# Two more stages of the first MLP compute their third token tile's first layer by half-tile block products

## The chip, the cores and the metric

The kernel runs on one core of one Trainium2 chip. The metric is the device time of one execution, in microseconds (us). The kernel before takes 558.34 us (median of 3 runs, 557.42 to 559.12). In what follows PE is TensorE, DVE is VectorE, ACT is ScalarE, POOL is GpSimd and SP is the engine whose queue issues most of the loads.

## The reference

Retention attention gives `x`, a matrix of 1536 tokens by 512, and two MLPs follow it. All inputs are float64 in memory; the result is float32.

```
for each of the 12 blocks of 64 positions:             # 2 batches, 8 heads of 64
    out[block] = ((qb kb^T) * Dmask) vb + (qb * lam_pow) kv_state
    kv_state   = lam_block * kv_state + (kb * rev_pow)^T vb
x = out as [1536, 512]
h = max(x @ w_in, 0);  x = (h * h) @ w_out             # first MLP,  w_in [512, 2048], w_out [2048, 512]
h = x @ w_in2;  out = max(0.01 h, h) @ w_out2          # second MLP, same sizes
```

## The kernel before

**Products.** A fp32 value is kept as a pair of fp32r values, a high part (`hi`, `xhi`, `g0h`) and the remainder (`lo`, `xlo`, `g0l`). One product is three matmuls that add up in PSUM: hi·hi, hi·lo and lo·hi. All of them are issued in `three` (L612).

**Tiles and stages.** The head of the program does retention in 12 units of 128 tokens. Then each MLP `l` (0 or 1) runs in four stages `s` of 512 of the 2048 hidden columns; a stage is written (l, s). The tokens are three tiles of 512, called tile 0, 1 and 2. A stage does in this order:

- `first_pair`: the first layer of tiles 0 and 1 together, as one 2 by 2 block product computed by seven block products and sums (a Strassen-like scheme) in place of eight. It needs sums of weight blocks (`sw`) and of token blocks (`tt`: `t2`, `t3`, `t4`). For each half `h` of the stage's columns the products go to PSUM banks A, B, C and D; `s1[h]` is a copy of bank A made on ACT (L758), `s2[h]`, `r22[h]` and the rest are sums made on DVE (`plus`, L752). `put` hands a finished block to `activate` (L530 to L541): ReLU, square, and the split into `g0h`/`g0l` (tile 0) or `g1h`/`g1l` (tile 1). The subtraction for the low part is L541 on DVE.
- `second` of tile 0: the second layer, 4 outputs of 12 matmuls. Its result is copied from PSUM (L798 on ACT) and added to a spill area in DRAM by a GpSimd DMA.
- the first layer of tile 2: `first`, 48 matmuls of 512 columns, in MLP 0; `first_halves` in MLP 1, which splits tile 2 into two halves of 256 tokens and uses seven block products again: 7 products x 2 halves of the hidden columns x 6 matmuls = 84 matmuls of 256 columns. `halves_sums` makes the sums of token blocks (`u2`, `u3`, `u4`, and one in place in `xhi[2]`/`xlo[2]`).
- `second` of tile 1 and of tile 2.

Stage (0,3) ends with tile 2's first layer placed among the second layer of tile 1.

**Weights.** A fetch (`fetch`, L65 on SP) brings 1 MB of float64 words into one of two `raw` buffers. `converting` (L131 to L177) turns it into a pair: an absolute value on ACT (L143), four DVE steps in place in one of two `hb` buffers (L146, L147, L149, L152), a cast to the high part on ACT (L168) and a subtraction for the low part on DVE (L170). The last of the four DVE steps frees the `raw` buffer, so the next fetch is issued behind it. W1 halves additionally get their block sums (`weight_sums`, or `sums_in_place` for stages after (1,0)). W2 halves go to one of three places `w2h0` to `w2h2` in turn up to stage (1,0); a place is free when the second layer that reads it is done.

**What sets the order.** PE's order is the program's own (a manual schedule). The other engines' orders come from the tile scheduler: it goes by program order and by priority; `tc.keep_in_program_order` pins an instruction. The conversions are generators; a `yield` in the parts of a stage lets `convert` take one step of the oldest conversion or, if fewer than two are at work, begin another. A set `opened` holds a conversion back until a buffer's former reader is placed. Every instruction waits in its engine's queue behind the one ahead of it.

Of the kernel before, what the change touches and what calls it, by code (L numbers as in the profile page):

```python
# [20 lines left out]
def tile_retention_then_two_mlps(  # L21
# [56 lines left out]

    order = [(0, 0, 0, 0), (0, 0, 0, 1), (0, 0, 1, 0), (0, 0, 1, 1)]
    stages = [(l, s) for l in range(2) for s in range(NS)]  # L80
    halved = (1, 0)
    for before, stage in zip(stages, stages[1:]):
        if before != stages[0]:
            order.append((*before, 1, 1))
        own = [(*stage, 1, 0), (*stage, 0, 0), (*stage, 0, 1)]
        order += own[1:] + own[:1] if stage > halved else own
    order.append((*stages[-1], 1, 1))
    todo = list(order)
    fetched, at_work = [], []
# [42 lines left out]
    def converting(pin):  # L132
        key, r = fetched.pop(0)
        l, s, n, h = key
        k = 4 if n == 0 else 2
        words = r.bitcast(U32).rearrange("p (f t) -> p f t", t=2)
        w_lo, w_hi = words[:, :, 0], words[:, :, 1]
        ve = nc.vector
        hb = cv.tile([P, 4 * CW], U32, tag="hb", name="hb", bufs=2)
        hf = hb.bitcast(F32)  # L140
        half = hb.bitcast(U16).rearrange("p (f t) -> p f t", t=2)[:, :, 0]

        step = nc.scalar.activation(hf, w_hi.bitcast(F32), AF.Abs)  # L143
        if pin or key == order[1]:
            tc.keep_in_program_order(step)
        yield ve.tensor_scalar(out=hf, in0=hf, scalar1=2.0 ** -15, scalar2=122368.0, op0=ALU.max, op1=ALU.min)  # L146
        yield ve.tensor_scalar(out=hb, in0=hb, scalar1=3, scalar2=0x3FFFFFFF,  # L147
                               op0=ALU.logical_shift_left, op1=ALU.bitwise_and)
        yield ve.scalar_tensor_tensor(out=hb, in0=w_hi, scalar=0xC0000000, in1=hb,  # L149
                                      op0=ALU.bitwise_and, op1=ALU.bitwise_or)  # L150

        step = ve.scalar_tensor_tensor(out=half, in0=w_lo, scalar=2.0 ** -29, in1=half, op0=ALU.mult, op1=ALU.add)  # L152
        fetch()
        yield step
        if (l, s) != stages[0] and n == 0 and (l, s) <= halved:
# [9 lines left out]
        place = (2 * stages.index((l, s)) + h) % 3 if (l, s) <= halved else (2, 0)[h]  # L165
# [5 lines left out]
        if n == 0 and (l, s) > halved:  # L171
            yield from sums_in_place(key, f"sw{h}", hf)
        if (l, s) == stages[-1] and n == 1:
            while ("sums", h) not in opened:
                yield None
            parts = spare if h else None
            yield from sums_in_place(key, "t2", hf, parts)  # L177

    def convert(pin=False):
        for piece in list(at_work):  # L180
            step = next(piece[1], False)
            if step is False:
                at_work.remove(piece)
            elif step is not None:
                if pin:
                    tc.keep_in_program_order(step)
                return
        if fetched and len(at_work) < 2:
            begin(pin)

    def begin(pin=False):
        key = fetched[0][0]
        at_work.append((key, converting_halves() if key == order[0] else converting(pin)))
        step = next(at_work[-1][1])
        if pin:
            tc.keep_in_program_order(step)
# [11 lines left out]
    def retention(ctx_att, att):  # L208
# [180 lines left out]
        for i in range(n_units):  # L389
# [23 lines left out]
                output(i, range(2, NP))  # L413
            else:
                state(i)
                for _ in range({8: 2, 9: 2, 10: 1}.get(i, 0)):
                    convert(pin=True)
                output(i)
            if i + 1 < n_units:
                scale_k(i + 1)  # L420
            if i == 11:
# [90 lines left out]
    def halves_sums(j):  # L512
# [8 lines left out]
        for n, src in ((2, c), (4, d), (1, a), (3, b)):  # L521
# [3 lines left out]
            if j == 0:  # L525
                pool, tag = {2: (wp, "w2h1"), 3: (wp, "w2l1"), 4: (cv, "rb")}[n]
                uu[n] = pool.tile([P, 2, 2, TT // 2], F32R, tag=tag, name=f"u{n}", bufs=1)
            split(uu[n][:, 0, j], uu[n][:, 1, j], src)

    def activate(l, src, r, ghi, glo, one=False):  # L530
        if l == 0 and one:
# [113 lines left out]
    def first_halves(l, s, t=2):  # L645
# [65 lines left out]
            sums_last(2)  # L711
        else:
            opened.update((*stages[stages.index((l, s)) + 1], 0, h) for h in range(2))


    def first_pair(l, s):
        last = (l, s) == stages[-1]
        new_g(l, s, 0)
        new_g(l, s, 1)
        ve = nc.vector  # L720
# [21 lines left out]
        def put(h, src, r, i, t):  # L742
            m = 2 * h + i
            with tc.high_priority(offset=400 if t == 0 else 0):
                if last:
                    activate_last(t, m, src)
                else:
                    activate(l, src, r, g[t][0][:, m], g[t][1][:, m], src is r and (l, s) != stages[1])

        def plus(h, out, where, other):  # L750
            with tc.high_priority(offset=400):
                ve.tensor_tensor(out=out, in0=ps[h, where], in1=other, op=ALU.add)  # L752

        both = range(2)
        for h in both:
            b = product(h, "A", "A11", "B11")
            s1[h] = plain()
            nc.scalar.copy(s1[h], b)  # L758
            yield (l, s) != stages[1]
        for h in both:  # L760
            product(h, "B", "S2", "T2")
            s2[h] = plain()
            plus(h, s2[h], "B", s1[h])
            yield (l, s) != stages[1]
        for h in both:
            product(h, "D", "A22", "T4")
            yield (l, s) != stages[1]
        if last:
            opened.add(("sums", 0))
        for h in both:  # L770
# [6 lines left out]
        for h in both:  # L777
            product(h, "C", "S1", "T1")
            plus(h, r22[h], "C", r22[h])
            yield (l, s) != stages[1]  # L780
        for h in both:
            put(h, product(h, "A", "A12", "B21", False), plain(), 0, 0)
            yield last
# [4 lines left out]
        for h in both:  # L788
            put(h, r22[h], r22[h], 1, 1)
            put(h, s2[h], s2[h], 0, 1)  # L790
        if last:
            sums_last(0)
            sums_last(1)
# [104 lines left out]
    def second(l, s, t, ms=range(4)):  # L898
        last = s == NS - 1
        for m in ms:  # L900
# [34 lines left out]
                opened.add(("pair", l, s))  # L935
            if t == 2 and m == 3:
                i = stages.index((l, s))
                mid = stages.index(halved)
                then = ((i + 1, 1), (i + 2, 0)) if i < mid - 1 else ((i + 1, 0), (i + 1, 1))
                opened.update((*stages[n], 1, h) for n, h in then)  # L940
            if (l, s, t) == (1, 0, 0) and m < 2:
                halves_sums(m)
            yield not (last and t == 1 and m > 1)

    def stage(l, s):
# [7 lines left out]
                            second(l, s, 2)]  # L953
        if (l, s) == stages[-1]:
            return parts + [first_halves(l, s)] + [second_last(s, t) for t in range(NTILE)]
        tile_2 = first_halves if l else first
        return parts + [second(l, s, 0), tile_2(l, s, 2), second(l, s, 1), second(l, s, 2)]

    begin()
# [1 line left out]
    with tc.manual_schedule(engines={mybir.EngineType.PE}):  # L961
        for l, s in stages:
            for part in stage(l, s):
                for room in part:
                    if room is not False:
                        convert(pin=(l, s) == stages[1])


# [23 lines left out]
```

## Time and profile before

| what | value |
|---|---|
| median of three runs | 558.34 us |
| the profiled execution | 558.2 us |
| span in its trace | 556.4 us |
| PE busy / DVE busy / ACT busy | 549.7 / 436.2 / 300.3 us |
| matmuls of `three` (L612), without a gap in the chain | 2472 |
| POOL busy | 87.8 us |

The span is what the trace of the profiled execution covers; 1.8 us of that execution lie around it. Busy time is that in which an engine has an instruction at work; matmuls overlap, so a start-to-start distance says more of PE than the length of one. A timeline row gives the start, the length, the engine, the line, what is written and what is read, and in brackets the idle time before it and what ended it.

### The profile page before, as it was taken

The numbers are of one execution on the slowest core, as the hardware profiler recorded it, in microseconds if no ns is written. First come the engines' busy times: TensorE is split into PE (matmuls) and PEld (weight loads), VectorE is DVE, ScalarE is ACT, GpSimd is POOL, SyncE is SP. The second block draws the span as 40 slices with busy tenths as digits, with TensorE's granted clock in tenths as the row PEclk, the third lists the DMA queues.
The fourth block names the chain that finished last, engine by engine and source line by source line (L and its number), as shares of the span: only waits on it lengthen the run. The fifth ranks groups of instructions, "written<-read, shape, count | busy, mean of one in ns | idle before, by whom it ended". The sixth has DMA issues, their size and how long they took to land.

```text
span 556.4 us, 8706 instructions
## 1 busy us (share of the span) xinstructions
PE 549.7 (99%) x3386; PEld 471.2 (85%) x3386; DVE 436.2 (78%) x643; ACT 300.3 (54%) x482; POOL 87.8 (16%) x99
## 2 busy tenths in 40 slices
PE   8999999999999999999999999999999999999997
PEld 7998888888888888888888889888898889888997
DVE  5668999996776895639999986969276964967987
ACT  3444799546783456553366374654364464646620
POOL 4965000000203101220000000000213011220041
PEclk9999999999999999999999999999999999999999
DMA  9998245443459716584413221263628643660434
GB/s 211 226 228 249 77 151 171 182 140 114 58 170 181 195 12 142 143 157 137 151 57 115 76 95 58 75 227 121 96 30 164 196 99 54 74 78 1 165 139 151
DMA packets 68056, 71.86 MB, mean 129 GB/s; under 512 B 39856, under 2 KB 43952, under 8 KB 68016
## 3 DMA queue, kind: packets, MB, share of 16 engines
q1 hardware_dynamic: 60816, 58.60, 33.8%
q0 software_dynamic: 6912, 12.59, 16.1%
q8 instruction: 26, 0.43, 0.3%
q10 hardware_dynamic: 288, 0.14, 0.1%
q14 instruction: 14, 0.11, 0.1%
HBM read 49.29 MB, written 22.02 MB: 128 GB/s over the span
## 4 chain that ended last, share of the span: by engine, by line
PE 96%; DVE 2%; DMA 1%; ACT 1%; issue 0%; SPq 0%; DVEq 0%; ACTq 0%
PE ps L612 90%; PE ps L301 2%; PE ps L363 1%; PE ps L361 1%; PE ps L280 1%; DMA k<-in_k 1%; PE ps L332 1%; DVE Pm L306 0%; ACT kqT L284 0%; DVE xlo L69 0%; DVE hb L124 0%; DVE st L344 0%; ACT kqT L288 0%; SPq L65 0%; DVE hb L128 0%
## 5 line engine op out<-in xcount | busy, mean ns | idle before, releaser
L802 POOL DMA_DIRECT2D spill<-f x48 | 42.6, 893 | 402.3 <-ACT f L798 402.3
L798 ACT COPY f<-ps 128x512 f32<-128x512 f32 x72 | 41.7, 586 | 68.3 <-PE ps L612 68.1
L612 PE MATMUL ps<-xlo,w1h 128*128 128x512 f32 (+1 forms) x190 | 69.3, 368 | 0.0
L612 PE MATMUL ps<-xhi,w1h 128*128 128x512 f32 (+1 forms) x184 | 68.3, 371 | 0.0
L612 PE MATMUL ps<-xhi,w1l 128*128 128x512 f32 (+1 forms) x184 | 68.2, 371 | 0.0
L752 DVE TENSOR_TENSOR f<-ps,f 128x512 f32<-128x512 f32 x70 | 46.0, 689 | 5.9 <-PE ps L612 5.7
L612 PE MATMUL ps<-xhi,sw 128*128 128x512 f32 (+1 forms) x176 | 49.6, 350 | 0.0
L170 DVE TENSOR_TENSOR w2l<-hb,w2h 128x1024 fp32r<-128x1024 f32 x16 | 19.6, 1222 | 34.0 <-ACT w2h L168 33.8
L612 PE MATMUL ps<-g0l,w2h 128*128 128x512 f32 x112 | 43.8, 391 | 0.0
L612 PE MATMUL ps<-g0h,w2l 128*128 128x512 f32 x112 | 43.6, 389 | 0.0
L612 PE MATMUL ps<-g0h,w2h 128*128 128x512 f32 x112 | 43.6, 389 | 0.0
L152 DVE SCALAR_TENSOR_TENSOR hb<-raw,hb 128x1024 uint16<-128x1024 uint32 x31 | 42.3, 1365 | 0.3
L541 DVE TENSOR_TENSOR g0l<-f,g0h 128x512 fp32r<-128x512 f32 x52 | 35.2, 689 | 7.6 <-ACT f L537 6.6
L612 PEld LDWEIGHTS ps<-xlo,w1h 128*128 128x128 f32 x190 | 35.5, 189 | 6.0
L612 PE MATMUL ps<-t,sw 128*128 128x512 f32 x168 | 40.4, 389 | 0.0
L612 PEld LDWEIGHTS ps<-xhi,w1h 128*128 128x128 f32 x184 | 34.7, 188 | 6.3 <-issue 0.2
L612 PEld LDWEIGHTS ps<-xhi,w1l 128*128 128x128 f32 x184 | 34.7, 188 | 6.0
L612 PE MATMUL ps<-w2h,g0h 128*128 128x512 f32 (+1 forms) x104 | 39.6, 381 | 0.0
L612 PE MATMUL ps<-w2l,g0h 128*128 128x512 f32 (+1 forms) x104 | 39.6, 381 | 0.0
L612 PE MATMUL ps<-w2h,g0l 128*128 128x512 f32 (+1 forms) x104 | 39.6, 381 | 0.0
L143 ACT ACTIVATE hb<-raw 128x1024 f32<-128x1024 f32 x31 | 35.2, 1146 | 7.9 <-DMA raw<-in_moe_w_out 2.4
L149 DVE SCALAR_TENSOR_TENSOR hb<-raw,hb 128x1024 uint32<-128x1024 uint32 x31 | 37.9, 1221 | 0.5
(220 smaller groups left out, 1326.9 us busy)
## 6 DMA issues: line engine op xcount, KB each, us to landing
raw<-in_moe_w_out SPq DMA_DIRECT2D x16, 1024.0 KB, 4.9
raw<-in_moe_w_in SPq DMA_DIRECT2D x15, 1024.0 KB, 6.3
spill<-f POOLq DMA_DIRECT2D x48, 256.0 KB, 4.3
spill<-f SPq DMA_DIRECT2D x24, 256.0 KB, 2.0
k<-in_k SPq DMA_DIRECT2D x12, 256.0 KB, 4.3
q<-in_q SPq DMA_DIRECT2D x12, 256.0 KB, 4.4
v<-in_v SPq DMA_DIRECT2D x12, 256.0 KB, 4.5
f<-spill SPq DMA_DIRECT2D x12, 256.0 KB, 2.7
```

Of the source, the lines that this page charges most:

```text
L143: step = nc.scalar.activation(hf, w_hi.bitcast(F32), AF.Abs)
L149: yield ve.scalar_tensor_tensor(out=hb, in0=w_hi, scalar=0xC0000000, in1=hb, op0=ALU.bitwise_and, op1=ALU.bitwise_or)
L152: step = ve.scalar_tensor_tensor(out=half, in0=w_lo, scalar=2.0 ** -29, in1=half, op0=ALU.mult, op1=ALU.add)
L170: yield ve.tensor_tensor(out=lo, in0=hf, in1=hi, op=ALU.subtract)
L280: nc.tensor.transpose(ps[half][:, p] if early else two[half][:, n, p], src[r, 2 * p:2 * p + 2, :].rearrange("s h d -> s (h d)"), ident[r, r])
L301: nc.tensor.matmul(raw_scores[i][par][:, p, :], kT[i][r, p, :], qT[i][r, p, :], start=True, stop=True)
L332: nc.tensor.matmul(ps[par * D:(par + 1) * D, p, :], kd[:, p, par, :], vn[:, 2 * p + par, :], start=True, stop=True)
L541: nc.vector.tensor_tensor(out=glo, in0=r, in1=ghi, op=ALU.subtract)
L612: nc.tensor.matmul(ps, a, b, start=start and n == 0, stop=stop and n == len(ops) - 1, skip_group_check=again)
L752: ve.tensor_tensor(out=out, in0=ps[h, where], in1=other, op=ALU.add)
L798: nc.scalar.copy(f, src)
L802: nc.gpsimd.dma_start(dst, f, accum_op=ALU.add)
```

## The change

**Tile 2 by halves.** Stages (0,1) and (0,2) use `first_halves` for tile 2, as MLP 1 does. `halves_sums(0)` is called at the start of (0,1)'s `first_pair` and `halves_sums(1)` at its end; `block_again(j)`, new, restores the block of `xhi[2]`/`xlo[2]` that had been overwritten, among the second layer of tile 1 of stage (0,2). `u2` and `u3` live in the third W2 place (`w2h1`, `w2l1`) and `u4` in `rb`, so W2 has two places in those stages (a table `places`).

**Weight sums and fetch order.** A list `in_place`, stages (0,2), (0,3), (1,1), (1,2) and (1,3), says which stages fetch W1 ahead of W2 and make W1's sums in place; before, those were (1,1) to (1,3).

**Conversion steps.** `convert` can be told to take steps of running conversions without beginning one (`"steps"`), or to begin one with its absolute value pinned (`"held"`). The yields of `first_pair` use it: in (0,2) none begins a conversion, from (0,3) on most begin it pinned; in (0,1) they let `convert` in neither before nor now.

**Squares.** For tile 1 the square of `put` goes back from DVE (L532) to ACT.

**Head.** At retention unit 9 one conversion step is taken in place of two, and one more is taken after the output of unit 10.

The diff, cut to what carries this:

```
-    halved = (1, 0)
+    halved = [stages[n] for n in (1, 2, 4, 5, 6, 7)]
+    in_place = [stages[n] for n in (2, 3, 5, 6, 7)]
+    places = ((0, 1), (2, 0), (2, 0), (1, 2), (0, 2), (2, 0), (2, 0), (2, 0))
...
-        order += own[1:] + own[:1] if stage > halved else own
+        order += own[1:] + own[:1] if stage in in_place else own
...
-    def convert(pin=False):
+    def convert(pin=False, start=True):
...
-        if fetched and len(at_work) < 2:
-            begin(pin)
+        if fetched and start and len(at_work) < 2:
+            begin(pin, hold=start == "held")
...
-                for _ in range({8: 2, 9: 2, 10: 1}.get(i, 0)):
+                for _ in range({8: 2, 9: 1, 10: 1}.get(i, 0)):
                     convert(pin=True)
                 output(i)
+                if i == 10:
+                    convert(pin=True)
...
+    def block_again(j):
+        of = []
+        for cs in (slice(0, TT // 2), slice(TT // 2, TT)):
+            of.append(plain()[:, 0:TT // 2])
+            nc.vector.tensor_tensor(out=of[-1], in0=xhi[2][:, j, cs], in1=xlo[2][:, j, cs], op=ALU.add)
+        nc.vector.tensor_tensor(out=of[1], in0=of[0], in1=of[1], op=ALU.add)
+        split(xhi[2][:, j, cs], xlo[2][:, j, cs], of[1])
...
-                    activate(l, src, r, g[t][0][:, m], g[t][1][:, m], src is r and (l, s) != stages[1])
+                    activate(l, src, r, g[t][0][:, m], g[t][1][:, m], src is r and (l, s) != stages[1] and t == 0)
...
+        if (l, s) == stages[1]:
+            halves_sums(0)
         for h in both:
             b = product(h, "A", "A11", "B11")
             s1[h] = plain()
             nc.scalar.copy(s1[h], b)
-            yield (l, s) != stages[1]
+            yield ("steps", "held")[h] if roomy else (l, s) == stages[2] and "steps"
...
+        if (l, s) == stages[1]:
+            halves_sums(1)
...
-        tile_2 = first_halves if l else first
+        tile_2 = first_halves if (l, s) in halved else first
...
-                        convert(pin=(l, s) == stages[1])
+                        convert(pin=(l, s) == stages[1], start=room != "steps" and (room or True))
```

Three places of the order follow. In a row stand the line, the operation, what is written and what is read, each with its number in the program; line numbers are larger in the changed kernel by the lines that it adds (L152 there is L154, L752 is L767).

**The head, DVE.** `st1` is the state of a batch that the next unit's output on PE reads, `hb_874` the first weight half under conversion, `xlo2` the low part of tile 2. Before:

```order
L344 TENSOR_TENSOR st0_143<-ps_947,tmp_956 64x4x64 x2
L126 SCALAR_TENSOR_TENSOR hb_874<-raw_683,hb_874 128x4x128
L128 SCALAR_TENSOR_TENSOR hb_874<-raw_683,hb_874 128x4x128
L69 TENSOR_TENSOR xlo2_898<-ps_963,xhi2_897 128x4x128
L306 TENSOR_TENSOR Pm_994<-ps_984,powers_126 128x512
L306 TENSOR_TENSOR Pm_994<-ps_985,powers_126 128x512
L344 TENSOR_TENSOR st1_145<-ps_997,tmp_1006 64x4x64 x2
L130 TENSOR_TENSOR w1l0_876<-hb_874,w1h0_875 128x4x128
```

and now:

```order
L346 TENSOR_TENSOR st0_143<-ps_947,tmp_956 64x4x64 x2
L128 SCALAR_TENSOR_TENSOR hb_874<-raw_683,hb_874 128x4x128
L69 TENSOR_TENSOR xlo2_898<-ps_962,xhi2_897 128x4x128
L308 TENSOR_TENSOR Pm_993<-ps_983,powers_126 128x512
L308 TENSOR_TENSOR Pm_993<-ps_984,powers_126 128x512
L346 TENSOR_TENSOR st1_145<-ps_996,tmp_1005 64x4x64 x2
L130 SCALAR_TENSOR_TENSOR hb_874<-raw_683,hb_874 128x4x128
L69 TENSOR_TENSOR xlo2_898<-ps_1011,xhi2_897 128x4x128
L132 TENSOR_TENSOR w1l0_876<-hb_874,w1h0_875 128x4x128
```

The conversion's last step (L128, now L130) stands behind the state update instead of ahead of it.

**Stage (0,1)'s `first_pair`, ACT and then DVE.** In the changed kernel `raw_1597` is a W1 half of stage (0,2) and `hb_1659` the buffer in which it is converted; numbers are given anew in each program, so they do not match across the two. `f_1692` and `f_1701` in the changed kernel are `s1[0]` and `s1[1]`, `f_1674` and `f_1683` in the one before. ACT before:

```order
L798 COPY f_1636<-ps_1622 128x512
L168 CAST w2h0_1606<-hb_1566 128x1024
L798 COPY f_1656<-ps_1640 128x512
L758 COPY f_1674<-ps_1667 128x512
L168 CAST w2h1_1659<-hb_1619 128x1024
L758 COPY f_1683<-ps_1676 128x512
```

and now:

```order
L817 COPY f_1636<-ps_1622 128x512
L170 CAST w2h0_1606<-hb_1566 128x1024
L817 COPY f_1656<-ps_1640 128x512
L145 ACTIVATE hb_1659<-raw_1597 128x1024
L775 COPY f_1692<-ps_1685 128x512
L68 CAST xhi2_897<-f_1666 128x256
L775 COPY f_1701<-ps_1694 128x512
```

The absolute value (L145) stands ahead of both `s1` copies; the cast of a second W2 half is gone from here. DVE before:

```order
L170 TENSOR_TENSOR w2l0_1607<-hb_1566,w2h0_1606 128x1024
L152 SCALAR_TENSOR_TENSOR hb_1619<-raw_1493,hb_1619 128x1024
L170 TENSOR_TENSOR w2l1_1660<-hb_1619,w2h1_1659 128x1024
L752 TENSOR_TENSOR f_1692<-ps_1685,f_1674 128x512
L752 TENSOR_TENSOR f_1701<-ps_1694,f_1683 128x512
```

and now:

```order
L172 TENSOR_TENSOR w2l0_1607<-hb_1566,w2h0_1606 128x1024
L154 SCALAR_TENSOR_TENSOR hb_1619<-raw_1493,hb_1619 128x1024
L520 TENSOR_TENSOR f_1666<-xhi2_897,xlo2_898 128x512
L520 TENSOR_TENSOR f_1668<-xhi2_897,xlo2_898 128x512
L491 TENSOR_TENSOR f_1666<-f_1666 128x256
L148 TENSOR_SCALAR hb_1659<-hb_1659 128x1024
L492 TENSOR_TENSOR f_1666<-f_1668,f_1666 128x256
L767 TENSOR_TENSOR f_1710<-ps_1703,f_1692 128x512
L493 TENSOR_TENSOR f_1668<-f_1668,f_1666 128x256
L69 TENSOR_TENSOR xlo2_898<-f_1666,xhi2_897 128x256
L767 TENSOR_TENSOR f_1719<-ps_1712,f_1701 128x512
```

The sums of `halves_sums` (L520, L491 to L494, L69) and the conversion's first step (L148) stand ahead of and between the two `plus` of `s2` (L752, now L767).

**Stage (0,2)'s `first_pair`, DVE.** `w2l2` is the low part of a W2 half that waits for its place, `raw_1871` and `raw_2027` hold what is converted next to it. Before:

```order
L152 SCALAR_TENSOR_TENSOR hb_2036<-raw_1924,hb_2036 128x1024
L170 TENSOR_TENSOR w2l2_2134<-hb_1996,w2h2_2133 128x1024
L170 TENSOR_TENSOR w2l0_2151<-hb_2036,w2h0_2150 128x1024
L146 TENSOR_SCALAR hb_2163<-hb_2163 128x1024
L147 TENSOR_SCALAR hb_2163<-hb_2163 128x1024
L149 SCALAR_TENSOR_TENSOR hb_2163<-raw_2027,hb_2163 128x1024
L752 TENSOR_TENSOR f_2173<-ps_2166,f_2148 128x512
```

and now:

```order
L172 TENSOR_TENSOR w2l2_2196<-hb_2125,w2h2_2195 128x1024
L154 SCALAR_TENSOR_TENSOR hb_2165<-raw_1871,hb_2165 128x1024
L172 TENSOR_TENSOR w2l0_2225<-hb_2165,w2h0_2224 128x1024
L767 TENSOR_TENSOR f_2235<-ps_2228,f_2210 128x512
L148 TENSOR_SCALAR hb_2359<-hb_2359 128x1024
L767 TENSOR_TENSOR f_2244<-ps_2237,f_2222 128x512
L149 TENSOR_SCALAR hb_2359<-hb_2359 128x1024
L151 SCALAR_TENSOR_TENSOR hb_2359<-raw_2156,hb_2359 128x1024
L148 TENSOR_SCALAR hb_2399<-hb_2399 128x1024
L154 SCALAR_TENSOR_TENSOR hb_2359<-raw_2156,hb_2359 128x1024
L767 TENSOR_TENSOR f_2266<-ps_2228,f_2210 128x512
```

The step that frees a `raw` buffer (L152, now L154, of `hb_2165`) stands behind `w2l2` instead of ahead of it, and the first step of a second new half (`hb_2399`) stands ahead of a `plus`.

## Rows read from the trace of the kernel before

**Rows 1.** Page, part 1: busy us, share of the span, instructions

```profile
PE 549.7 (99%) x3386; PEld 471.2 (85%) x3386; DVE 436.2 (78%) x643; ACT 300.3 (54%) x482; POOL 87.8 (16%) x99
```

**Rows 2.** Chain of waits: start us, length us, engine, line, count

```profile
54.66 498.22 PE ps L612 x2472
```

**Rows 3.** Timeline of PE, first layer of tile 2: (0,1), then (1,0)

```profile
150.12 0.39 PE L612 MATMUL ps<-xhi,w1h 128*128 128x512 f32 x1
...
161.00 0.39 PE L612 MATMUL ps<-g1h,w2h 128*128 128x512 f32 x1
...
337.94 0.28 PE L612 MATMUL ps<-xhi,w1h 128*128 128x256 f32 x1
...
348.01 0.40 PE L612 MATMUL ps<-w2h,g1h 128*128 128x512 f32 x1
```

**Rows 4.** Timeline of DVE and PE at the end of the head

```profile
48.90 1.04 DVE L128 SCALAR_TENSOR_TENSOR hb<-raw,hb 128x512 uint16<-128x512 uint32 x1
...
52.24 0.78 PE L361 MATMUL ps<-qS,st 128*64 128x128 f32 x3 [0.75 <-DVE st L344]
```

**Rows 5.** Stage (0,1), SP's timeline and the landing of that load

```profile
120.17 0.38 SPq L65 DMA_DIRECT2D raw<-in_moe_w_in  x1
...
raw<-in_moe_w_in SPq DMA_DIRECT2D x1, 1024.0 KB, 6.1
```

**Rows 6.** Loads: (0,2) at 176.21, (0,3) at 253.10, then the page's medians

```profile
raw<-in_moe_w_in SPq DMA_DIRECT2D x1, 1024.0 KB, 9.3
...
raw<-in_moe_w_out SPq DMA_DIRECT2D x1, 1024.0 KB, 4.8
...
raw<-in_moe_w_in SPq DMA_DIRECT2D x15, 1024.0 KB, 6.3
```

**Rows 7.** Instructions by line and form: busy us, mean ns, idle before

```profile
L143 ACT ACTIVATE hb<-raw 128x1024 f32<-128x1024 f32 x31 | 35.2, 1146 | 7.9 <-DMA raw<-in_moe_w_out 2.4 <-DVE w1l L170 2.3 <-DVE f L752 1.6
L146 DVE TENSOR_SCALAR hb<-hb 128x1024 f32<-128x1024 f32 x31 | 21.4, 689 | 5.2 <-ACT hb L143 5.0
```

**Rows 8.** Stage (0,1), timelines of DVE, ACT and PE

```profile
123.75 1.34 DVE L152 SCALAR_TENSOR_TENSOR hb<-raw,hb 128x1024 uint16<-128x1024 uint32 x1
...
127.36 1.28 DVE L752 TENSOR_TENSOR f<-ps,f 128x512 f32<-128x512 f32 x2
...
131.24 0.64 ACT L535 ACTIVATE f<-f 128x512 f32<-128x512 f32 x1 [4.58 <-DVE f L752]
...
128.21 2.91 PE L612 MATMUL ps<-t,sw 128*128 128x512 f32 x12
...
139.34 0.46 PE L612 MATMUL ps<-g0l,w2h 128*128 128x512 f32 x1
```

**Rows 9.** Stage (0,2), timelines of DVE and PE

```profile
182.46 2.58 DVE L170 TENSOR_TENSOR w2l<-hb,w2h 128x1024 fp32r<-128x1024 f32 x2 [6.32 <-ACT w2h L168]
...
191.91 0.44 DVE L453 TENSOR_TENSOR rb<-hb 128x256 f32<-128x256 f32 x1
192.25 1.24 DVE L149 SCALAR_TENSOR_TENSOR hb<-raw,hb 128x1024 uint32<-128x1024 uint32 x1
193.38 2.50 DVE L752 TENSOR_TENSOR f<-ps,f 128x512 f32<-128x512 f32 x4
...
199.98 0.71 DVE L541 TENSOR_TENSOR g0l<-f,g0h 128x512 fp32r<-128x512 f32 x1
...
202.02 0.39 PE L612 MATMUL ps<-g0l,w2h 128*128 128x512 f32 x1
```

**Rows 10.** Stage (0,3), timelines of DVE and PE

```profile
262.51 0.70 DVE L541 TENSOR_TENSOR g0l<-f,g0h 128x512 fp32r<-128x512 f32 x1
...
264.58 0.39 PE L612 MATMUL ps<-g0l,w2h 128*128 128x512 f32 x1
...
299.26 0.50 PE L612 MATMUL ps<-g0l,w2h 128*128 128x512 f32 x1
```

**Rows 11.** Windows, stage (0,1): busy PE, PEld, DVE, ACT, POOL; clock

```profile
120.04:159.90 39.86, 39.86 (x177) 32.65 (x176) 30.72 (x43) 27.59 (x46) 3.65 (x4) 1.00 0.49 121
```

More of the change, by code (lines that the diff above doesn't have):

```diff
@@ L154, in converting @@
         yield step
-        if (l, s) != stages[0] and n == 0 and (l, s) <= halved:
+        if (l, s) != stages[0] and n == 0 and (l, s) not in in_place:
             w = hf.rearrange("p (k f) -> p k f", k=k)
@@ L164, in converting @@
             yield None
-        place = (2 * stages.index((l, s)) + h) % 3 if (l, s) <= halved else (2, 0)[h]
+        place = places[stages.index((l, s))][h]
         tags = (f"w1h{h}", f"w1l{h}") if n == 0 else (f"w2h{place}", f"w2l{place}")
@@ L170, in converting @@
         yield ve.tensor_tensor(out=lo, in0=hf, in1=hi, op=ALU.subtract)
-        if n == 0 and (l, s) > halved:
+        if n == 0 and (l, s) in in_place:
             yield from sums_in_place(key, f"sw{h}", hf)
@@ L187, in convert, with begin @@
                 return
-        if fetched and len(at_work) < 2:
-            begin(pin)
-    def begin(pin=False):
+        if fetched and start and len(at_work) < 2:
+            begin(pin, hold=start == "held")
+    def begin(pin=False, hold=False):
         key = fetched[0][0]
-        at_work.append((key, converting_halves() if key == order[0] else converting(pin)))
+        at_work.append((key, converting_halves() if key == order[0] else converting(pin or hold)))
         step = next(at_work[-1][1])
@@ L713, in first_halves @@
             opened.update((*stages[stages.index((l, s)) + 1], 0, h) for h in range(2))
+            if (l, s) == (0, 2):
+                opened.add((0, 3, 1, 0))
     def first_pair(l, s):
         last = (l, s) == stages[-1]
+        roomy = (l, s) > stages[2]
         new_g(l, s, 0)
@@ L763, in first_pair @@
             plus(h, s2[h], "B", s1[h])
-            yield (l, s) != stages[1]
+            yield roomy and "held"
         for h in both:
             product(h, "D", "A22", "T4")
-            yield (l, s) != stages[1]
+            yield roomy and "held"
         if last:
@@ L779, in first_pair @@
             plus(h, r22[h], "C", r22[h])
-            yield (l, s) != stages[1]
+            yield roomy and "held"
         for h in both:
@@ L937, in second @@
                 i = stages.index((l, s))
-                mid = stages.index(halved)
-                then = ((i + 1, 1), (i + 2, 0)) if i < mid - 1 else ((i + 1, 0), (i + 1, 1))
-                opened.update((*stages[n], 1, h) for n, h in then)
+                opened.update((*stages[n], 1, h) for n, h in ((i + 1, 0), (i + 1, 1), *[(4, 0)] * (i == 2)) if n < len(stages))
             if (l, s, t) == (1, 0, 0) and m < 2:
                 halves_sums(m)
+            if (l, s, t) == (0, 2, 1) and m < 2:
+                block_again(m)
             yield not (last and t == 1 and m > 1)
```

## The prediction

> **What bounds the kernel now.** I read the page first: PE is busy for 99% of the span, DVE for 78% and ACT for 54% [rows 1]. Then the chain of waits: from 54.66 us on it is one row, 2472 matmuls of L612 in 498.22 us [rows 2]. The reader is to see that PE hardly waits once the head is over, so matmul time that goes is gained, and a new wait of PE is lost in full. Which wait could arise I read from the timelines of PE, DVE and ACT side by side, at the places where PE takes something that DVE or ACT has made just before.
>
> **Matmul time.** Tile 2's first layer in stage (0,1) runs from 150.12 to 161.00: 10.88 us for 48 matmuls, 0.227 each. The half-tile form in (1,0) runs from 337.94 to 348.01: 10.07 us for 84 matmuls of half the width, 0.120 each [rows 3]. So a stage gains 0.81 us and the two stages 1.6. The granted clock is 1.00 in this stage [rows 11], and PE stays as busy, so I price both forms at these distances. The Trainium skill (TensorE: Matmul & The Clock Gate, section Back-to-back issue gap) has N/2.4 + 2.5 ns for a matmul of N columns at full clock; by that the estimate would be 215.8 and 109.2 ns, 1.19 us a stage and 2.4 in all, and the time below 0.8 lower. The rows show wider distances for both, and I go by them.
>
> **Head.** Before, DVE's L128 (1.04 us from 48.90) stands ahead of the state update L344, and PE waits 0.75 us at 52.24 for that [rows 4]. Now it stands behind it. The state comes 1.04 earlier, PE's wait goes, and what is late next is the first weight pair that L612 begins with, for its conversion step is now later: L130, one L69 and L132 follow the state update, where before only L130 did. The gain is bounded by 1.1 (the step and some) and, if the weight pair is late by the length of one L69, by 0.4. I take 1.0, near the step's own length, since PE has the outputs of the last unit to do in between.
>
> **A, `first_pair` of (0,1).** The absolute value of a new half stands in ACT's queue ahead of the `s1` copies, and DVE's L148 behind it ahead of `s2`. The load is issued at 120.17 and lands 6.1 us later [rows 5], at 126.27; SP's and DVE's order ahead of it are as before, so it is issued then too. The absolute value takes 1.15 [rows 7] and ends at 127.4. DVE is ready for L148 before: L154 ends at 125.1 [rows 8], two sums of 512 columns at 0.60 (193.38, four in 2.50) and one of 256 at 0.34 (191.91 to 192.25) [rows 9] bring it to 126.65. So it waits 0.8 there. Then L148 (0.69 long, taken as 0.60 as the next follows on it [rows 7]), one sum of 0.34 and `s2` of 0.69 end at 129.1 to 129.2. PE took the product that needs that bank at 128.21; before, DVE had the first of its two L752 from 127.36 done some 0.2 earlier [rows 8]. PE waits 1.0.
> Then the splits of the token sums stand among the `plus`: from 129.2 on there are six steps of 256 columns (2.04) and three of 512 (1.80) up to the sum with which ACT begins the ReLU: 133.05 instead of 131.24. Of these 1.8 late, PE's own wait covers 1.0; 0.8 to 0.9 is left, and the chain that begins there had no room: the matmul at 139.34 that takes its low part took 0.46 instead of 0.39 [rows 8]. ACT has the copies to do in that time but no other wait. A costs 1.0 + 0.9 = 1.9. If the load landed in 4.8 us, as the nearest fast row has it [rows 6], it is there before DVE comes: L148 at 126.65, `s2` at 128.3, a wait of 0.1 and the later 0.85, so 1.0. Below nothing it cannot go, since everything added stands ahead of what PE took without room.
>
> **B, `first_pair` of (0,2).** The second new W1 half of (0,3) can be fetched only when L154 of `hb_2165` has freed a buffer. That step now stands behind `w2l2`, which waits for its place: before, DVE stood idle 6.32 us for it and began at 182.46 [rows 9]. The place comes free with the end of (0,1)'s second layer, as before. With 1.25 for `w2l2` and 1.34 for L154 [rows 8] the fetch is issued at 185.0. What is queued behind on DVE is `s2`, the ReLU's sums and `g0l`. A median load takes 6.3 [rows 6]: 191.3, the absolute value to 192.5, and DVE, whose other work ahead of L148 of that half is some 4.7 us from 185.0, waits for it. From there to the `g0l` that PE took at 202.02 there are, in the new order, 12 steps of 512 columns at 0.60, two conversion steps of 0.60, L151 at 1.13 (192.25 to 193.38) and L154 at 1.3: 10.85, so 203.4, and 0.1 for the length of the last. PE waits 1.5; before, 199.98 + 0.71 left it 1.33 of room [rows 9]. At 4.8 us for the load the wait is nothing; at 9.3, which the load issued at 176.21 in this stage took [rows 6], it is 4.5.
>
> **C, (0,3).** Likewise the absolute value of a second half stands ahead of the ACT copies that feed `g0l`. Before, L541 ended at 263.21 and PE took it at 264.58, 1.37 of room [rows 10]. The load before at this place took 4.8 [rows 6]: then no wait. With 6.3 the copies wait until about 260.6 and two conversion steps stand ahead of that `g0l`: some 1.7 to 2 later. I take 0.6, between 0 and, with a load of 9.3, 2.5.
>
> **D, end of (0,3).** The matmul at 299.26 took 0.50, 0.11 over the usual 0.39 [rows 10]: its low part came just late, so there is no room. Conversion steps moved into DVE's queue ahead of it would show whole, one of them 0.6 and several up to 1.0; a reordering could also take them away. I take 0.4, from 0 to 1.0.
>
> **What costs nothing.** `halves_sums` adds 2 x (2 x 0.60 + 8 x 0.34) = 7.8 us to DVE. DVE is busy for 30.72 of the 39.86 us from 120.04 on, so 9.1 are idle [rows 11], and outside A the sums are due only when tile 2 begins. Without that cover they would cost up to 7.8. Tile 1's squares take ACT 0.6 more each, and ACT is busy 27.59 of the same 39.86. `block_again` lies under the second layer, where PE needs nothing of DVE. MLP 1 and the tail are as before.
>
> **Sum.** -1.6 - 1.0 + 1.9 + 1.5 + 0.6 + 0.4 = +1.8, on the profiled execution's 558.2 (span 556.4 and 1.8 around it), which is 0.14 under the median of the runs shown: 560.0.
>
> **Rivals.**
> *Fast loads.* If all these loads land in 4.8 us, A costs 1.0, B and C nothing, D 0.4: -2.6 + 1.4 = -1.2, 557.0. For it: the row of 4.8 at (0,3). Against it: 6.1 at the very place of A and the median of 6.3. The Trainium skill (DMA: Bandwidth & Descriptors, section Anatomy of one DMA) fits 2.0 us and bytes over 436e9 a second, though for the GpSimd path; for 1 MB that estimate is 4.4 us, which would give this rival's time. No 1 MB row here is that short.
> *Hidden.* The scheduler's added steps all fall into DVE's 9.1 idle us and PE finds what it needs: only -1.6 - 1.0, 555.6. For it: 7.8 fits into 9.1. Against it: the idle time lies behind PE's products, and the order shows the steps ahead of `s2`, where 0.2 was left.
> *One late load, slower by much.* The load of B takes 9.3, as the neighbouring one did beside the spill traffic: B 4.5, and the sum is +4.8, 563.0. Between -1.2 at 4.8 and +1.8 at 6.3 the sum crosses nothing at a load of some 5.4; from there on it ends slower. Against it: one row against a median of 6.3.
> *The half tiles are no gain in MLP 0.* Were matmuls of 256 columns spaced at 10.88 / 84 = 0.130 beside the denser DVE, each stage would lose its 0.81: 561.6. The rows of (1,0) speak against it, so I give it little.
>
> **Chances.** Forecast 0.45, its own range 558.8 to 561.5; fast loads 0.24; hidden 0.15; one late load 0.12; no gain 0.04. A measurement of this kernel tells 0.3% from no change, 1.7 us: faster is below 556.7, slower above 560.0. Of the forecast some six tenths are slower (0.26), the rest within; with the late load and the last rival slower is 0.41. Fast loads are mostly within (0.17); with the forecast's rest that is 0.36. Hidden and the faster part of the fast loads make 0.23. The range reaches from hidden to the late load, 555.6 to 563.0.
>
> **What would show it.** In the changed trace PE has a gap of about 1.0 before the product with `t4` near 128, the release from a DVE sum, and DVE one before L148 that ends with the absolute value. A second gap of some 0.9 stands ahead of the first `g0l` of (0,1), one of 1.5 ahead of (0,2)'s, one smaller in (0,3). Tile 2's first layer takes 10.07 in (0,1) and (0,2), and the wait of 0.75 in the head is gone. I am wrong if the loads land so early that DVE finds the absolute values done, or if DVE's idle time takes up the steps without a gap of PE.

## The result and the profile after

The changed kernel takes 564.12 us (median of 6 runs, 563.04 to 565.32), the one before 557.44 beside it on the same chip (6 runs). The ratio is 1.0115, with a 95% interval of [1.0103, 1.0127]: slower by 6.4 us (6.7 between the two medians), where the forecast was 1.8 slower and the range ended at 563.0. The profiled execution took 563.65 (span 561.9), 5.45 more than that of before.

Part 1 of the page of the changed kernel, in the columns of [rows 1], has PE at 98% instead of 99%, with 72 more matmuls and only 1.1 us more of busy time:

```profile
PE 550.8 (98%) x3458; PEld 473.2 (84%) x3458; DVE 447.8 (80%) x673; ACT 309.9 (55%) x510; POOL 87.7 (16%) x99
```

The waits of PE in its trace are the first thing to read (engine, line, what it waits for; us in total, times, longest). Six waits within the MLPs stand there, three for a sum and three for a low part, where [rows 2] had 2472 matmuls without one:

```profile
PE ps L624 <- DVE f L767: 2.1, 3, 1.0
PE ps L624 <- DVE g0l L553: 2.0, 3, 1.0
```

PE's timeline says where they are. The first five rows are stage (0,1), the next four (0,2), the last two (0,3):

```profile
128.53 0.73 PE L624 MATMUL ps<-t,sw 128*128 128x512 f32 x2 [0.41 <-DVE f L767]
...
140.31 0.51 PE L624 MATMUL ps<-g0l,w2h 128*128 128x512 f32 x1 [0.38 <-DVE g0l L553]
...
142.11 0.50 PE L624 MATMUL ps<-g0l,w2h 128*128 128x512 f32 x1
...
151.54 0.28 PE L624 MATMUL ps<-xhi,w1h 128*128 128x256 f32 x1
...
161.61 0.40 PE L624 MATMUL ps<-g1h,w2h 128*128 128x512 f32 x1
...
200.89 0.50 PE L624 MATMUL ps<-xhi,sw 128*128 128x512 f32 x1 [1.02 <-DVE f L767]
...
204.18 0.40 PE L624 MATMUL ps<-g0h,w2h 128*128 128x512 f32 x1
205.63 0.50 PE L624 MATMUL ps<-g0l,w2h 128*128 128x512 f32 x1 [1.05 <-DVE g0l L553]
205.96 0.39 PE L624 MATMUL ps<-g0h,w2l 128*128 128x512 f32 x1
...
266.84 0.50 PE L624 MATMUL ps<-xhi,sw 128*128 128x512 f32 x1 [0.72 <-DVE f L767]
...
304.67 0.50 PE L624 MATMUL ps<-g0l,w2h 128*128 128x512 f32 x1 [0.56 <-DVE g0l L553]
```

Tile 2 in (0,1) takes 161.61 - 151.54 = 10.07, as forecast. The idle figure tells less than a wait costs. From 204.18 to 205.63 it is 1.45 instead of 0.227, and the next matmul is 0.33 behind instead of 0.227: some 1.3 lost where the bracket says 1.05, since the overlap of neighbouring matmuls goes too. So the table goes by distances from start to start, not by brackets. Each row is one stretch of PE, before and after; the differences are taken before rounding:

| stretch | before | after | difference | forecast |
|---|---|---|---|---|
| (0,1), `first_pair` and second layer of tile 0 (A) | 30.07 | 31.75 | +1.67 | +1.9 |
| (0,2), the same (B) | 29.92 | 33.02 | +3.10 | +1.5 |
| (0,3), the same (C) | 29.92 | 31.64 | +1.72 | +0.6 |
| end of (0,3): second layer of tile 2 (D) | 11.02 | 11.78 | +0.76 | +0.4 |
| tile 2 of (0,1) and (0,2) | 21.76 | 20.14 | -1.62 | -1.6 |
| from the first MLP matmul to tile 2's second layer in (1,3) ("body") | 488.04 | 493.71 | +5.67 | |

The rest of the body changes by +0.03. The MLPs begin 0.23 earlier; that start lies between 53.0 and 54.6 in the profiled executions of all versions, so one profile does not show what the head gained. In this one the wait for the state is gone, but PE waits 0.56 for a load of `v` at 46.57, which it did not before.

For A, the timelines of SP, ACT and DVE read as forecast: the load issued at 119.82 lands in time for an absolute value at 125.67, and L148 comes 0.59 after DVE was free, ahead of the sum that PE takes.

```profile
125.67 1.14 ACT L145 ACTIVATE hb<-raw 128x1024 f32<-128x1024 f32 x1 [4.25 <-DMA raw<-in_moe_w_in]
...
126.84 0.69 DVE L148 TENSOR_SCALAR hb<-hb 128x1024 f32<-128x1024 f32 x1 [0.59 <-ACT hb L145]
127.79 0.68 DVE L767 TENSOR_TENSOR f<-ps,f 128x512 f32<-128x512 f32 x1
```

For B, DVE's timeline up to and in (0,2), to be laid beside [rows 9]. Its first row begins the weight sums made in place (L480 to L485), its second the next conversion:

```profile
168.21 0.43 DVE L480 TENSOR_TENSOR hb<-hb 128x256 f32<-128x256 f32 x1
...
177.60 0.69 DVE L148 TENSOR_SCALAR hb<-hb 128x1024 f32<-128x1024 f32 x1
...
183.03 1.23 DVE L151 SCALAR_TENSOR_TENSOR hb<-raw,hb 128x1024 uint32<-128x1024 uint32 x1
184.17 1.22 DVE L172 TENSOR_TENSOR w2l<-hb,w2h 128x1024 fp32r<-128x1024 f32 x1
185.31 1.33 DVE L154 SCALAR_TENSOR_TENSOR hb<-raw,hb 128x1024 uint16<-128x1024 uint32 x1
...
194.72 0.69 DVE L148 TENSOR_SCALAR hb<-hb 128x1024 f32<-128x1024 f32 x1 [2.03 <-ACT hb L145]
```

Before, that conversion's first step (L146) began here:

```profile
168.10 0.69 DVE L146 TENSOR_SCALAR hb<-hb 128x1024 f32<-128x1024 f32 x1
```

The chain that ends with PE's second wait in (0,2) (start, length, what):

```profile
185.31 1.34 DVE hb L154
186.71 6.76 DMA raw<-in_moe_w_in
193.56 1.14 ACT hb L145
...
195.33 1.35 DVE hb L154
...
202.64 1.13 DVE hb L151
...
205.63 0.50 PE ps L624
```

The 6.32 idle us ahead of `w2l2` are gone: it follows directly on a conversion step. The windows of both kernels show the same (stretch, its length, then the busy time of PE, PEld, DVE, ACT and POOL, the granted clock, the share of DMA and GB/s). Before, DVE was busy for 11.96 of 21 us:

```profile
161.00:182.00 21.00, 21.00 (x94) 17.41 (x93) 11.96 (x14) 10.43 (x15) 6.51 (x7) 1.00 0.77 173
```

and now for 15.03:

```profile
161.00:182.00 21.00, 21.00 (x97) 17.51 (x96) 15.03 (x21) 13.75 (x21) 5.47 (x7) 1.00 0.52 64
```

### The profile page after: what moved, and what is told of

It reads as the page before. It is cut to its first block, busy times and chain, and to the rows that moved or that the text cites. A ratio compares the mean times of both kernels' runs of the same rounds, so it can differ in the third digit from the quotient of the medians.

```text
span 561.9 us, 8908 instructions
## 1 busy us (share of the span) xinstructions
PE 550.8 (98%) x3458; PEld 473.2 (84%) x3458; DVE 447.8 (80%) x673; ACT 309.9 (55%) x510; POOL 87.7 (16%) x99
## 4 chain that ended last, share of the span: by engine, by line
PE 68%; DVE 16%; DMA 7%; ACT 5%; issue 3%; SPq 0%; ACTq 0%; DVEq 0%
PE ps L624 61%; DMA raw<-in_moe_w_in 4%; PE ps L303 2%; DVE hb L154 2%; DVE hb L151 2%; DVE f L767 2%; PE ps L365 2%; DVE g0l L553 2%; PE ps L363 1%; ACT f L547 1%; DMA raw<-in_moe_w_out 1%; ACT hb L145 1%; DVE hb L148 1%; PE ps L334 1%; DMA v<-in_v 1%
## 5 line engine op out<-in xcount | busy, mean ns | idle before, releaser
L624 PE MATMUL ps<-xlo,w1h 128*128 128x512 f32 (+1 forms) x174 | 61.3, 356 | 0.0
L624 PE MATMUL ps<-xhi,w1h 128*128 128x512 f32 (+1 forms) x168 | 60.4, 360 | 0.0
L624 PE MATMUL ps<-xhi,w1l 128*128 128x512 f32 (+1 forms) x168 | 60.3, 359 | 0.0
L624 PE MATMUL ps<-xhi,sw 128*128 128x512 f32 (+1 forms) x208 | 56.7, 342 | 1.9 <-DVE f L767 1.7
L694 DVE TENSOR_TENSOR f<-ps,f 128x512 f32<-128x512 f32 x30 | 20.7, 691 | 44.7 <-ACT f L699 26.5
L767 DVE TENSOR_TENSOR f<-ps,f 128x512 f32<-128x512 f32 x70 | 46.6, 684 | 4.9 <-PE ps L624 4.6
L145 ACT ACTIVATE hb<-raw 128x1024 f32<-128x1024 f32 x31 | 35.1, 1143 | 18.9 <-DMA raw<-in_moe_w_in 12.9
L624 PEld LDWEIGHTS ps<-xhi,sw 128*128 128x128 f32 x208 | 36.9, 190 | 7.4 <-DVE f L767 3.2
L154 DVE SCALAR_TENSOR_TENSOR hb<-raw,hb 128x1024 uint16<-128x1024 uint32 x31 | 42.3, 1364 | 0.2
L624 PEld LDWEIGHTS ps<-t,sw 128*128 128x128 f32 x168 | 31.5, 188 | 7.3 <-DVE f L767 0.8
L624 PEld LDWEIGHTS ps<-xlo,w1h 128*128 128x128 f32 x174 | 32.6, 189 | 4.9
```

What stands on the lines that cost most here:

```text
L624: nc.tensor.matmul(ps, a, b, start=start and n == 0, stop=stop and n == len(ops) - 1, skip_group_check=again)
L694: nc.vector.tensor_tensor(out=out, in0=ps[where], in1=other, op=ALU.add)
```

## The experiments

The theory (the order): the waits come from where conversion steps and fetches stand in the queues of DVE and ACT. The rival (the capacity): DVE, with the sums of the half tiles, and ACT, with the squares, have too much to do. Times below are medians, each ratio is to runs of the kernel before beside them.

**The order alone.** The changed kernel with tile 2 of (0,1) and (0,2) as it was:

```
-    halved = [stages[n] for n in (1, 2, 4, 5, 6, 7)]
+    halved = [stages[n] for n in (4, 5, 6, 7)]
...
-            halves_sums(0)
...
-            halves_sums(1)
...
-                block_again(m)
```

> The changed kernel without its half-tile products in (0,1) and (0,2), and so without the token sums and block_again; every other edit stays (head, squares, weight sums in place, fetch order, conversion control). Theory ORDER: PE's waits come from the place of the conversion steps and of the absolute values (which wait for loads) ahead of the sums that PE needs. Then most of the waits of (0,2), (0,3) and its end stay, 3 to 4 us of the 5.6 there, a few tenths of the 1.7 of (0,1), and the 1.6 of matmul time is lost again: 559.5 to 561 us. Rival CAPACITY: DVE and ACT cannot hold the 7.8 us of token sums; without them the waits vanish and the time is that of the kernel before less the head's gain, 556.5 to 557.5.

Measured 561.34, ratio 1.0058 [1.0043, 1.0073], body 491.86. That is a little above the 559.5 to 561 expected from the order. Of the waits, 2.4 us stay in B, 0.7 in C, 0.5 in A and 0.3 in D: 3.9 of the 7.3, without one added sum of tokens; DVE is busy for 431.2 us, less than the 436.2 of the kernel before. The chain there has a load of 9.27 us in B:

```profile
178.85 9.27 DMA raw<-in_moe_w_in
```

So the order costs by itself. In this order the half tiles cost more than they gain, too: the changed kernel's body is 1.85 longer than this one's, though its load in B is the shorter one (6.76).

**The head alone**, in the kernel before:

```
-                for _ in range({8: 2, 9: 2, 10: 1}.get(i, 0)):
+                for _ in range({8: 2, 9: 1, 10: 1}.get(i, 0)):
...
+                if i == 10:
+                    convert(pin=True)
```

> The kernel before with the head's edit alone (one conversion step at unit 9 instead of two, one after the output of unit 10). Theory ORDER: the 0.75 us wait for the state goes and nothing takes its place: 0.5 to 0.8 us faster than before. Rival: another wait of the head (a load of v, which PE waited 0.56 us for in the profiled run of the changed kernel) takes its place: within 0.3 us of before.

557.07, ratio 0.998 [0.9967, 0.9993], so -1.1 us (between -1.8 and -0.4), with a body of 487.98 (488.04 before). PE's wait for the state is gone and none takes its place; DVE's timeline has the state ahead of the conversion step:

```profile
50.96 0.87 DVE L344 TENSOR_TENSOR st<-ps,tmp 64x256 f32<-64x256 f32 x2
51.86 0.75 DVE L128 SCALAR_TENSOR_TENSOR hb<-raw,hb 128x512 uint16<-128x512 uint32 x1
```

**A taken away.** The W1 half that was begun in (0,1)'s `first_pair` is held until the second layer of tile 0, and the first `halves_sums` is moved to the end of the pair:

```
+    held = {(0, 2, 0, 1)}
...
+        if fetched and start and len(at_work) < 2 and fetched[0][0] not in held:
...
+        if t == 0 and l == 0:
+            held.discard({1: (0, 2, 0, 1), 2: (0, 3, 0, 1), 3: (1, 0, 0, 1)}.get(s))
```

> The changed kernel with stage (0,1)'s first_pair cleared only: the absolute value of the second W1 half of (0,2) may begin only after the pair, and the first token sums are made at its end together with the second. All work stays. Theory ORDER: (0,1) loses its 1.7 us of waits, (0,2) and (0,3) keep theirs: 562 to 562.8 us. Rival CAPACITY: the sums come late instead, PE waits for them in tile 2's first layer, and the time stays at 564 or above.

562.96, ratio 1.009 [1.0069, 1.0111], a little above the 562 to 562.8 expected. A goes from 31.75 to 30.29 (before 30.07): shown, for the two edits together. But B, which was to keep its wait, grows from 33.02 to 34.60. The load there took 10.3 us, ACT waits for it, DVE for ACT, and the sum L768 that stands behind DVE's step is late with it. DMA, ACT and DVE:

```profile
raw<-in_moe_w_in SPq DMA_DIRECT2D x1, 1024.0 KB, 10.3
```

```profile
189.20 1.12 ACT L146 ACTIVATE hb<-raw 128x1024 f32<-128x1024 f32 x1 [3.86 <-DMA raw<-in_moe_w_in]
```

```profile
186.03 0.68 DVE L768 TENSOR_TENSOR f<-ps,f 128x512 f32<-128x512 f32 x1
190.35 0.69 DVE L149 TENSOR_SCALAR hb<-hb 128x1024 f32<-128x1024 f32 x1 [3.64 <-ACT hb L146]
190.95 0.68 DVE L768 TENSOR_TENSOR f<-ps,f 128x512 f32<-128x512 f32 x1
```

**All three pairs cleared.** The same for the halves begun in (0,2) and (0,3), with the absolute value pinned where it is now begun:

```
+    held = {(0, 2, 0, 1), (0, 3, 0, 1), (1, 0, 0, 1)}
...
-                        convert(pin=(l, s) == stages[1], start=room != "steps" and (room or True))
+                        convert(pin=(l, s) in stages[1:4], start=room != "steps" and (room or True))
```

> The changed kernel with all three pairs cleared: the second W1 half of the next stage is begun only after the pair in (0,1), (0,2) and (0,3), the conversions of these stages are pinned to their place in the program, and the first token sums of (0,1) are made at the end of its pair. All work stays. Theory ORDER: the 6.4 us of waits in the three pairs go, the 0.8 at the end of (0,3) may stay: 556 to 558 us. Rival CAPACITY: the conversions come too late instead and PE waits for weights or sums elsewhere: 561 us or more.

558.83, ratio 1.001 [0.9999, 1.0021], body 489.28: the half tiles' sums are all there and 4.4 of the body's 5.7 us are gone, but the time is above the 556 to 558 expected from the order. B is 30.01. A load of 10.9 us fell into (0,2) here too, but nothing that PE takes stood behind it. What is left is 0.2 in A, C (0.96) and D, which grows to 1.6. There DVE is busy for 26.19 of 26.20 us:

```profile
282.70:308.90 26.20, 24.77 (x109) 20.19 (x108) 26.19 (x40) 16.94 (x28) 0.00 (x0) 1.00 0.40 130
```

where it was, before, for 23.34 of 24.60:

```profile
283.40:308.00 24.60, 24.60 (x109) 20.19 (x108) 23.34 (x34) 17.60 (x27) 0.00 (x0) 1.00 0.31 97
```

**B alone**, with only (0,3,0,1) held and the conversions of (0,2) pinned to their place:

```
+    held = {(0, 2, 0, 0): (0, 3, 0, 1)}
...
+                        convert(pin=(l, s) in stages[1:3], start=room != "steps" and (room or True))
```

> The changed kernel with stage (0,2)'s first_pair cleared only: the second W1 half of (0,3) is begun only after the pair, and the conversions of (0,2) are pinned to their place in the program. (0,1) and (0,3) stay as in the changed kernel. Theory ORDER: the 3.1 us of waits of (0,2) go and little comes back: 561 us or 3 less than the changed kernel. Rival POSTPONED: as when (0,1) was cleared alone, where (0,2) grew by what (0,1) lost, the moved conversions show up later in (0,3), and the time falls by less than 1.

560.06, ratio 1.0035 [1.0019, 1.0052]. B's 3.10 becomes 0.09. C goes from 1.72 to 0.96 although nothing of (0,3) was held, so nearly half of C was inherited from B, and holding (1,0,0,1) does nothing for the rest. D grows to 1.5 here as well, although nothing was changed there.

**D to POOL.** As the kernel with all pairs cleared, with the sums of tokens in (0,3) on another engine:

```
-                        token_sums(m - 2)
+                        token_sums(m - 2, nc.gpsimd)
```

> The version with all three pairs cleared (558.8 us), and the eight subtractions of the token sums in (0,3) done on POOL instead of DVE. DVE loses 8 x 0.6 = 4.8 us there. Rival CAPACITY for the end of (0,3): the 1.6 us of wait there goes to below 0.4: 557.3 us. Theory ORDER: the low parts that need POOL's slower sums (1.3 to 1.8 us each in the rows of POOL) stand in DVE's queue ahead of the low part that PE waits for, and the wait stays or grows: 558.8 or more.

565.38, ratio 1.0127 [1.0108, 1.0146]; D is 18.61. A subtraction that takes some 0.7 on DVE takes 1.30 to 3.87 on POOL, and DVE's `g0l` that runs beside one takes 1.75 instead of 0.69. POOL, then DVE:

```profile
277.90 3.87 POOL L492 TENSOR_TENSOR f<-f 128x512 f32<-128x512 f32 x1 [32.75 <-DVE f L944]
...
300.86 2.12 POOL L493 TENSOR_TENSOR f<-f 128x512 f32<-128x512 f32 x1 [6.78 <-issue]
```

```profile
301.77 1.75 DVE L554 TENSOR_TENSOR g0l<-f,g0h 128x512 fp32r<-128x512 f32 x1
```

DVE's instruction ends 0.54 after POOL's (303.52 and 302.98), so most of its usual 0.69 fell behind POOL's end. The Trainium skill (SBUF — State Buffer, section Who interferes with whom) says that a DVE instruction with two inputs in SBUF contends with a GpSimd instruction that reads SBUF; the two rows agree. Since the work on POOL took longer and held DVE up, this run does not tell whether DVE's load alone makes D.

**D by moving a conversion out, and by priority.** All pairs stay cleared. The second W2 half of (1,0), written (1,0,1,1), is held until the second layer of tile 2 in (0,3), `activate` of the first layer of tile 2 gets priority there, and the opening of the first W2 half, (1,0,1,0), moves from (0,2) into (0,3):

```
+    held = {(0, 1, 0, 0): (0, 2, 0, 1), (0, 2, 0, 0): (0, 3, 0, 1), (0, 3, 0, 0): (1, 0, 0, 1), (0, 3, 2, 1): (1, 0, 1, 1)}
...
+            with tc.high_priority(offset=400 if s == NS - 1 else 0):
+                activate(l, ps, plain(), ghi[:, m], glo[:, m])
...
+            if (l, s, t, m) == (0, 3, 0, 1):
+                opened.add((1, 0, 1, 0))
```

> The version with all three pairs cleared (558.8 us), with three further moves around the end of (0,3): the first W2 half of (1,0) is cast only after the pair, the second W2 half of (1,0) is begun only in the second layer of tile 2, and tile 2's first layer in (0,3) has priority on DVE and ACT. No work goes away. Theory ORDER: its last waits, 1.0 us in (0,3) and 1.6 at its end, go to below 0.5 in all: about 556.5 us, below the kernel before. Rival CAPACITY: DVE was busy for all of the last 26 us of (0,3), so what is moved comes late for (1,0) instead: 558 or more.

560.31, ratio 1.0042 [1.0025, 1.0058]. The time is on the side of the rival, 558 or more. D is gone (10.88), but C is 1.47 longer than before and tile 2's first layer in (1,0) takes 12.33 instead of 10.07. Its token sums now come last in queues that got the work:

```profile
PE ps L625 <- ACT u L68: 1.4, 1, 1.4
PE ps L625 <- DVE g0l L554: 0.8, 2, 0.5
PE ps L625 <- DVE u L69: 0.3, 1, 0.3
```

**The same without the moved opening, with priority for the token sums of (1,0):**

```
+                with tc.high_priority(offset=400):
+                    halves_sums(m)
```

> The version with all three pairs cleared (558.8 us), with the second W2 half of (1,0) begun only in the second layer of tile 2 of (0,3), priority on DVE and ACT for tile 2's first layer in (0,3), and now also for the token sums of (1,0), which came 2.3 us late in the last such version. Theory ORDER: of that version's waits, 1.2 us in the pairs stay, the 1.6 at the end of (0,3) go and nothing comes back in (1,0): from the first matmul of the MLPs to the last product 487.7 us, against 488.0 before and 493.7 in the changed kernel; time 556.5 to 557.2, below the kernel before by the head's 1.0 and a little. Rival CAPACITY: DVE is full from (0,3) into (1,0), and what is put off is missed later: 558.5 or more.

556.65 (12 runs), ratio 0.9974 [0.9961, 0.9986]: as expected from the order, and faster than both kernels by the interval, with a body of 487.73. The head's edit alone had 0.998, and the two intervals overlap, so what the half tiles add to it is read from the body: 0.31 less than before, of the 1.62 that their matmuls save. One wait for DVE is left, in C (0.98 by starts):

```profile
PE ps L625 <- DVE g0l L554: 0.7, 1, 0.7
```

DVE's timeline there has the low part of a W2 half, 1.23 long, between the sums and low parts of tile 0; PE waits for the `g0l` of 262.50:

```profile
260.17 1.23 DVE L173 TENSOR_TENSOR w2l<-hb,w2h 128x1024 fp32r<-128x1024 f32 x1
261.30 0.70 DVE L554 TENSOR_TENSOR g0l<-f,g0h 128x512 fp32r<-128x512 f32 x1
...
262.50 0.70 DVE L554 TENSOR_TENSOR g0l<-f,g0h 128x512 fp32r<-128x512 f32 x1
```

Before, both low parts of that stage were made ahead of all its sums:

```profile
245.02 2.59 DVE L170 TENSOR_TENSOR w2l<-hb,w2h 128x1024 fp32r<-128x1024 f32 x2 [12.74 <-ACT w2h L168]
```

**The squares.** Tile 1's squares on ACT in the kernel before:

```
-                    activate(l, src, r, g[t][0][:, m], g[t][1][:, m], src is r and (l, s) != stages[1])
+                    activate(l, src, r, g[t][0][:, m], g[t][1][:, m], src is r and (l, s) != stages[1] and t == 0)
```

> The kernel before with the squares of tile 1 in (0,2) and (0,3) on ACT, that edit alone. Theory ORDER: no change beyond 0.3 us, since neither engine sets a wait there in the kernel before. Rival: ACT's longer chain (two more steps of 0.6 in each half) makes the low parts late in (0,2) and (0,3): 0.5 to 1 us slower.

558.83, ratio 1.0011 [0.9996, 1.0026]: no difference that can be told. C grows by 0.27 there; B by 1.36, with one load of 11.8 us, so that part can't be put down to the squares. The reverse, the changed kernel with the squares back on DVE:

> The changed kernel with tile 1's squares back on DVE, that edit alone undone. If the squares on ACT are part of the loss (alone on the kernel before they went with 1.3 us more in (0,2), in a run in which one load took 11.8 us): 562.8 to 563.5. If they are not, DVE's longer queue in the pairs makes the waits of (0,2) and (0,3) longer by two to four steps of 0.6: 565 or more.

563.3, ratio 1.0088 [1.0066, 1.011]. This lies in the range expected if the squares were part of the loss (562.8 to 563.5), but the interval overlaps that of the changed kernel, and the body, 494.19, is 0.48 longer than its 493.71: C is 0.38 shorter, A and B together 0.53 longer. So the squares are at most a small part, in C; whether they cost anything in all is not shown.

## Why the prediction was right or wrong

**Matmul time: right**, 10.07 twice, so the distances seen in (1,0) hold beside the denser DVE too, and the rival without a gain is out.

**Head: right** by the kernel with that edit alone, -1.1 for the 1.0 forecast, without a wait for the first weight pair. In the profiled execution of the changed kernel only 0.23 of it shows.

**A: right in place and size** (1.67 for 1.9). I split it 1.0 and 0.9; by starts 0.7 falls at the product with `t4` and the rest at two low parts, at 140.31 and 142.11. Without the two edits to which I put it down, 0.2 is left.

**B: the step that failed is "the fetch is issued at 185.0".** I took the moment at which DVE reaches the freeing step from the trace of before, with DVE idle for 6.32 us and `w2l2` at 182.46. In the changed kernel two weight sums made in place stand ahead (168.21 to 177.68 in its chain), and the two conversions that DVE began at 168.10 before begin at 177.60. They fill the idle time, so `w2l2` begins at 184.17, not at 182.46 + 0.65 (the stage begins 0.65 later). That is 1.06, and by as much the fetch leaves later than forecast (186.71 for 185.65). The load then took 6.76 for 6.3, another 0.46. Together 1.5, which with the forecast 1.5 makes 3.0 of the 3.10; behind the absolute value the 10.85 that I had added up took 10.9 (194.7 to 205.6). I also looked for one gap, at the low part; more than half stands before it, 1.3 at a product that needs a bank (200.89) and 0.4 at 202.69. With that fetch's half held and the conversions pinned, 0.09 is left: shown, for the two together. That the fetch's moment is what counts within it is read from the chain; no run moved that alone.

**C: mis-sized for the same reason.** The freeing step stands at 256.25, 1.58 later than its place before (251.70) shifted by the 2.97 that PE was late by then. I had asked only for the length of the load (5.46 here), not for its issue. As in B, more than half (1.0) stands at a product that needs a bank (266.84), where I had looked only at the low part. Of the 1.72, 0.76 goes when B goes. The other 0.96 or more stays in all versions with B cleared; the squares alone gave 0.27. In the traces of those at 558.83, 560.06 and 556.65 the low part of a W2 half stands among tile 0's sums, as in the rows at 260.17 above; its 1.13 (260.17 to 261.30) is enough for the wait. No run takes that step out, so this is read from the trace and not shown.

**D: 0.76 for 0.4.** It was priced as an order without room, and it is that: DVE is full there, so what comes last is late, and priority for what PE takes, together with one W2 half put off, removes it. Where a second W2 half is put off too and the token sums of (1,0) have no priority, the wait appears in (1,0).

**The rivals.** *Hidden* failed as to place: 7.8 us of sums do fit beside PE (the version at 556.65 has them all, with D gone, A and B under 0.25 and C at 0.98), but not where this order put them. *Fast loads*: no load at these places was that short (5.8, 6.76 and 5.46). *One late load* came nearest in time (563.0) for the wrong reason here, so that is luck: B's load was not late by itself, its fetch was. In other versions it did happen (10.3 with B at 34.60).

**The sum.** -1.62 + 0.03 - 1.1 + 1.67 + 3.10 + 1.72 + 0.76 = +4.6, against 6.4 measured. Of the 1.8 between, 0.9 is the part of the head's 1.1 that the profiled execution does not show: with 0.23 there, the sum is the 5.45 between the two profiled executions. The other 0.9 stays open; that execution of the changed kernel was 0.47 below its median, that of the one before 0.76 above. The version with A taken away has the same body (493.76) at a ratio that makes 5.0 us, so the body doesn't explain it; whether loads in the executions that were not profiled were longer, no run shows.

## What to carry to other kernels

When a step is moved in a queue, work out anew when its engine reaches it: idle time seen in the old trace is the first thing that a reordering fills, and a fetch released by a late step is late by as much. Keep steps that wait for a load out of the queue ahead of what the bound engine takes next, and let them follow it; then a load of 10.9 us costs hardly anything (B at 30.01 for 29.92). Only then is any of a saving on the bound engine kept: the same half tiles stood in the kernel at 564.12 and in the one at 556.65, and even there the body keeps 0.31 of their 1.62.

## What the runs showed of the hardware

A 1 MB load on SP's queue took from 4.7 to 11.8 us from issue to landing. The two issued between 171 and 187 us, whose words are converted in (0,2), took 5.8 to 11.8 in the different versions, while the one issued near 119 us took 5.6 to 6.1 in every run.

After the gap of 3.83 us in the kernel with sums on POOL, PE's clock fell. Three windows of it (the clock is the third number from the right): PE had 0.45 us of work in the first, got 0.67 there and 0.51, the level of 1.2 GHz, for the next 4.1 us, with matmuls of 512 columns 0.43 apart, and full clock again behind it. Behind the wait of 1.05 us in the changed kernel the granted clock is 1.00, and from the second matmul on they stand 0.23 apart (205.96, 206.19).

```profile
299.30:303.50 4.20, 0.45 (x1) 0.13 (x1) 4.17 (x6) 2.46 (x4) 2.12 (x1) 0.67 0.17 52
303.50:307.60 4.10, 4.02 (x10) 3.16 (x11) 4.10 (x6) 1.32 (x2) 0.94 (x1) 0.51 0.10 23
307.60:312.00 4.40, 4.40 (x21) 3.65 (x20) 3.02 (x5) 1.76 (x3) 2.57 (x2) 1.00 0.63 217
```
